# Sinkhorn block attention and token mixer: one stationary matrix for both mixer projections, keys turned by TensorE, the second copy of the queries made by a DMA, and a new order of work with more filler matmuls

## The chip, the cores and the metric

One core of one Trainium2 chip. Times are device microseconds (us) of a whole execution, as medians of several. The profiler's span of one execution is about 1.8 us shorter than its time.

## The reference, cut to what matters

```python
P = sinkhorn(sort_net)                         # per batch (4) and head (8), 8 x 8
k_s = einsum('bhij,bhjcd->bhicd', P, k_b)      # sorted blocks of 96 tokens; v the same
attn = softmax(q_b @ k_s.T / 8)                # inside each block
x = concat_heads(attn @ v_s)                   # 4 x 768 x 512
wq, wk = x @ w_q, x @ w_k                      # 512 -> 64
mixed = einsum('bst,btd->bsd', wq @ wk.T / 8, x)
out = relu(mixed) @ w_out                      # float32
```

## The kernel before

A hand-written order lists units of work; each unit emits its instructions on TensorE (PE), its copy out of PSUM on ScalarE ("a") or VectorE ("d"), and its DMA. The first digit is the batch, the second the part. Q, K, V prepare queries and sorted keys and values; T regroups V by a DMA inside SBUF (VS to VT); S is scores and exponential; AV is the weighted sum; XT transposes; WQ and WK project; A is the small product of wk and x; MIX applies wq; OUT is the last product and the store. A trailing number puts that many filler matmuls, whose results nobody reads, in front of the unit.

```python
ORDER = """
    V00d3 V01a V02d V03a K01d K02a T00 K03a T04 K00d T03 T01 T02 T07 Q12d10 Q13a T06 S00a T05
    S01a S02a Q11d Q10d AV00d AV01d AV02d S03a S05a XT00d AV03d S04a S07a S06a AV04d XT01a V12d
    V11a AV07d WK00a WQ00a AV05d AV06d V13a K13a XT02d K11a ...
"""
# ... loads of inputs, all on GpSimd's queue because they cast float32 to bfloat16 ...
    def further_loads():                     # after the last regroup of batch 0
        load_v(1)
        make_m(1, PTR, nc.gpsimd)
        nc.gpsimd.dma_start(out=wqd[:, :, 0, :], in_=moe_w_q.rearrange("(t p) d -> p t d", p=P))
        nc.gpsimd.dma_start(out=wk_t, in_=moe_w_k.rearrange("(t p) d -> p t d", p=P))
        load_k(1)
        # ... w_out, q2 ...
        nc.gpsimd.tensor_copy(wqd[:, :, 1, :], wqd[:, :, 0, :])      # q weights twice
        # ... v2, k2, q3, v3, k3; three buffers each ...
# ...
    def u_WQ(b, h, eng):                     # q on partitions 0-63 and again on 64-127
        ps = psum1(hf)
        for pt in range(PT):
            nc.tensor.matmul(ps, wqd[:, pt].rearrange("p a d -> p (a d)"),
                             XT[b][:, pt, h * hf:(h + 1) * hf], ...)
        copies[eng](wqT[b][:, h * hf:(h + 1) * hf], ps)

    def u_WK(b, h, eng):                     # keys, tokens on the partitions: 4 x 4 matmuls
        for ii in range(n):
            for pt in range(PT):
                nc.tensor.matmul(ps[0:m, ii, :], XT[b][:, pt, i * BLK:i * BLK + m], wk_t[:, pt, :], ...)
        copies[eng](wkb[b][:, h * n:(h + 1) * n], ps[0:BLK])
```

The softmax here doesn't subtract the row's maximum and nothing guards it: scores larger than these inputs give would overflow.

## Time and profile before

| | before |
|---|---|
| time, median (3 runs) | 114.73 us (113.94 to 115.61) |
| span of the profiled run | 111.7 us |
| mean granted TensorE clock | 0.952 |
| TensorE matmuls | 1444 busy records, 83% of the span |
| ScalarE, VectorE | 67%, 62% |
| DMA engines | full until about 70 us, 0.6 busy to 73 |

In the rows of digits each digit is a fortieth of the span (2.8 us); a 9 is 90% or more. In the table by stretches, columns are busy time and number of instructions of PE, weight loads, VectorE, ScalarE and GpSimd, then clock, DMA share (as printed it can exceed 1) and GB/s. Modelled ends of matmuls overlap, so a unit is priced from one start to the next. The half-clock stretch can also be seen directly: the same AV unit before and inside it, in the timeline (start, duration, engine, line, operation, and in brackets idle time and what ended it):

```profile
24.27 0.44 PE L277 MATMUL ps<-VT,E 96*128 96x65 bf16 x8 [0.25 <-ACT E L265]
...
25.89 0.65 PE L277 MATMUL ps<-VT,E 96*128 96x65 bf16 x8
```

TensorE waits 0.25 us for an exponential, as it does ahead of each AV here; then the clock falls and eight matmuls take half as long again, with no idle time before them.

### The profile page before, as it was taken

To read this page: it belongs to the slowest core of one execution; us is meant where nothing else is said; L and a number is where in the kernel's file an instruction comes from. 1 tells how busy PE (TensorE), PEld (TensorE's weight loads), DVE (VectorE), ACT (ScalarE), POOL (GpSimd) and SP (SyncE) were. 2 spreads that over 40 slices of the span, in tenths; PEclk is the share of its full clock that TensorE was granted. 3 is DMA by queue.
4 is the path that set the end of the run, shared out by engine and by line. 5 is a ranking of instruction groups with operands and counts; after the bars stand their busy time and mean duration, and the time that the engine had idled before them with its cause. 6 is when DMAs were issued, how large, how long until landed. Compare 5 with 4: busy or idle time off the path is not lost.

```text
span 111.7 us, 3418 instructions
## 1 busy us (share of the span) xinstructions
PE 93.2 (83%) x1444; PEld 63.0 (56%) x1444; DVE 68.9 (62%) x154; ACT 75.2 (67%) x116; POOL 33.4 (30%) x54
## 2 busy tenths in 40 slices
PE   0007869977899999999998999999899999999930
PEld 0007326846576787665696688755478687334400
DVE  1586787498365736688897577858388874071000
ACT  4014637578743999849599895995968836885640
POOL 6950002999099900043210000003150000051030
PEclk9999999996555999999999999999999999999999
DMA  0999999999999999999999999602543000048772
GB/s 3 111 202 206 203 203 204 248 132 178 159 193 197 205 204 219 246 239 206 204 216 247 247 368 344 192 4 94 188 183 113 0 0 6 0 164 305 294 269 95
DMA packets 19758, 19.80 MB, mean 177 GB/s; under 512 B 2208, under 2 KB 17696, under 8 KB 19744
## 3 DMA queue, kind: packets, MB, share of 16 engines
q0 software_dynamic: 15696, 15.21, 73.1%
q1 hardware_dynamic: 4048, 4.38, 13.2%
q8 instruction: 11, 0.18, 0.7%
q14 instruction: 3, 0.02, 0.1%
HBM read 20.19 MB, written 6.29 MB: 237 GB/s over the span
## 4 chain that ended last, share of the span: by engine, by line
issue 40%; DMA 29%; POOL 14%; DVE 10%; ACT 1%; PE 1%; POOLq 1%; ACTq 0%
DMA Vn<-in_v_dram 23%; DMA wqd<-in_moe_w_q_dram 6%; POOL out_dram L362 5%; POOL Vn L115 2%; POOL M L217 2%; POOL VT L252 2%; DVE M L217 1%; DVE tmp L162 1%; POOL Qn L105 1%; DVE Pm L161 1%; ACT Pm L155 1%; DVE tmp L160 1%; DVE tmp L163 1%; DVE tmp L159 1%; DVE VS L244 1%
## 5 line engine op out<-in xcount | busy, mean ns | idle before, releaser
L362 POOL DMA_DIRECT2D out_dram<-ot x18 | 9.8, 547 | 59.7 <-ACT ot L360 34.4
L265 ACT ACTIVATE E<-ps 96x768 bf16<-96x768 f32 x32 | 24.0, 810 | 1.4 <-PE ps L260 1.3
L357 PE MATMUL ps<-wo_t,mixT 128*128 128x512 bf16 x96 | 23.1, 379 | 0.0
L284 DVE TENSOR_TENSOR X<-ps,R 96x512 bf16<-96x512 f32 x32 | 22.0, 687 | 1.1
L360 ACT COPY ot<-ps 128x512 f32<-128x512 f32 x20 | 11.8, 588 | 9.0 <-PE ps L357 8.9
L206 PE MATMUL ps<-idb,Qn 128*64 128x128 bf16 x192 | 8.5, 238 | 9.0 <-DMA Qn<-in_q_dram 8.8
L277 PEld LDWEIGHTS <-E 96*128 96x128 bf16 (+1 forms) x256 | 12.4, 108 | 5.2 <-ACT E L265 2.1
L277 PE MATMUL ps<-VT,E 96*128 96x65 bf16 (+1 forms) x256 | 14.0, 204 | 0.8 <-ACT E L265 0.7
L357 PEld LDWEIGHTS <-mixT 128*128 128x128 bf16 x96 | 8.6, 98 | 9.3 <-issue 0.9
L206 PEld LDWEIGHTS <-Qn 128*64 128x64 bf16 x192 | 6.8, 121 | 10.2 <-DMA Qn<-in_q_dram 9.0
L260 PE MATMUL ps<-QT,KT 64*128 64x96 bf16 x256 | 10.0, 211 | 1.4 <-DVE X L284 0.8
L244 ACT CAST VS<-ps 128x768 bf16<-128x768 f32 x11 | 8.8, 827 | 2.9 <-PE ps L241 2.9
L283 DVE RECIPROCAL R<-ps 96x8 f32<-96x8 f32 x32 | 6.3, 198 | 6.7 <-PE ps L277 6.6
L241 PE MATMUL ps<-Vn,M 128*128 128x384 bf16 x32 | 8.1, 361 | 1.7 <-DMA Vn<-in_v_dram 0.9
L260 PEld LDWEIGHTS <-KT 64*128 64x128 bf16 x256 | 7.0, 97 | 4.5 <-issue 1.6
L351 DVE TENSOR_SCALAR mixT<-ps 128x768 bf16<-128x768 f32 x7 | 6.7, 955 | 4.0 <-PE ps L344 3.9
L294 PE MATMUL ps<-idb,X 96*128 96x96 bf16 x128 | 8.3, 211 | 0.0
L234 ACT CAST KT<-ps 128x768 bf16<-128x768 f32 x10 | 7.8, 800 | 0.6 <-PE ps L230 0.5
L230 PE MATMUL ps<-M,Kn 128*64 128x128 bf16 x192 | 7.5, 223 | 0.2 <-DVE VS L244 0.2
L349 ACT ACTIVATE mixT<-ps 128x768 bf16<-128x768 f32 x9 | 7.2, 819 | 0.3 <-PE ps L344 0.3
L230 PEld LDWEIGHTS <-Kn 128*64 128x64 bf16 x192 | 6.1, 112 | 2.1 <-issue 1.0
L294 PEld LDWEIGHTS <-X 96*128 96x128 bf16 x128 | 6.6, 101 | 1.1
(71 smaller groups left out, 128.0 us busy)
## 6 DMA issues: line engine op xcount, KB each, us to landing
out_dram<-ot POOLq DMA_DIRECT2D x18, 256.0 KB, 2.6
Qn<-in_q_dram POOLq DMA_DIRECT2D x4, 768.0 KB, 14.7
Vn<-in_v_dram POOLq DMA_DIRECT2D x4, 768.0 KB, 12.0
Kn<-in_k_dram POOLq DMA_DIRECT2D x4, 768.0 KB, 15.1
VT<-VS SPq DMA_DIRECT2D x28, 97.5 KB, 5.5
out_dram<-ot SPq DMA_DIRECT2D x6, 256.0 KB, 2.0
wo_t<-in_moe_w_out_dram POOLq DMA_DIRECT2D x1, 512.0 KB, 11.7
VT<-VS POOLq DMA_DIRECT2D x4, 97.5 KB, 3.5
```

What stands on the lines that cost most here:

```text
L206: nc.tensor.matmul(ps[hh * D:(hh + 1) * D, r, :], Qn[b][:, 2 * kp + hh, r, :], idb, is_transpose=True, start=True, stop=True, skip_group_c ...
L230: nc.tensor.matmul(ps[hh * D:(hh + 1) * D, r * P:(r + 1) * P], Kn[b][:, h, r, :], Ms[b][:, h].rearrange("p s i -> p (s i)"), start=True, s ...
L241: nc.tensor.matmul(ps[:, hh, 0:R6 * D], Ms[b][:, h].rearrange("p s i -> p (s i)"), Vn[b][:, h].rearrange("p r d -> p (r d)"), start=True, ...
L244: copies[eng](VS[b % 2][:, :, 2 * kp:2 * kp + 2, 0:D].rearrange("p r h d -> p h r d"), ps[:, :, 0:R6 * D].rearrange("p h (r d) -> p h r d" ...
L260: nc.tensor.matmul(ps[:, hh, kp * BLK:(kp + 1) * BLK], KT[b][hh * D:(hh + 1) * D, k0:k0 + P], QT[b][hh * D:(hh + 1) * D, kp, :, i * SP:(i ...
L265: nc.scalar.activation(E.rearrange("p (a n) -> p a n", a=2), ps[0:BLK, :, 0:4 * BLK], ACT.Exp, scale=scale)
L277: nc.tensor.matmul(ps[0:m, h // 4, (h % 4) * D1:(h % 4 + 1) * D1], E[:, e * BLK:e * BLK + m], VT[b][:, i, h, :], start=True, stop=True, sk ...
L284: nc.vector.tensor_mul(Xb[b][:, i].rearrange("p (a t d) -> p a t d", a=2, t=4), pv[:, :, :, 0:D], Rt.unsqueeze(3).to_broadcast([BLK, 2, 4, ...
L294: nc.tensor.matmul(ps[:, pt, ii * BLK:(ii + 1) * BLK], Xb[b][:, 2 * j + ii, pt * P:(pt + 1) * P], idb[0:BLK, 0:BLK], is_transpose=True, st ...
L357: nc.tensor.matmul(ps, mixT[b][:, pt, r, :], wo_t[:, pt, :], start=(pt == 0), stop=(pt == PT - 1), skip_group_check=True)
L360: copies[eng](ot, ps)
L362: queue.dma_start(out=od[:, r, :], in_=ot)
```

## The change

The intent: compute keys and queries in one product (keys on partitions 0 to 63, queries on 64 to 127), turn the keys by four cheap matmuls against the identity, and fetch the second copy of the queries, which MIX needs on partitions 0 to 63, by a DMA inside SBUF (unit "D"). The two weights load right behind q1. The order was searched anew, with units "F" that emit only fillers.

```diff
+    for a, w in ((0, moe_w_k), (1, moe_w_q)):                 # right behind load_q(1)
+        nc.gpsimd.dma_start(out=wkq[:, :, a, :], in_=w.rearrange("(t p) d -> p t d", p=P))
     def further_loads():
-        nc.gpsimd.dma_start(out=wqd[:, :, 0, :], in_=moe_w_q...)
-        nc.gpsimd.dma_start(out=wk_t, in_=moe_w_k...)
-        nc.gpsimd.tensor_copy(wqd[:, :, 1, :], wqd[:, :, 0, :])
     def u_WQ:
-            nc.tensor.matmul(ps, wqd[:, pt]...
+            nc.tensor.matmul(ps, wkq[:, pt]...
+    def u_D(b, n, eng):
+        wq2[b] = rot.tile([DH, S], BF16, tag="wq2", name="wq2")
+        nc.sync.dma_start(out=wq2[b], in_=wT[b][DH:2 * DH, :])
     def u_WK:
-            for pt in range(PT):
-                nc.tensor.matmul(ps[0:m, ii, :], XT[b][:, pt, i * BLK:i * BLK + m], wk_t[:, pt, :], ...
+            nc.tensor.matmul(ps[0:m, ii, :], wT[b][:, i * BLK:i * BLK + m], idb[:, 0:DH], ...
+    def u_F(b, n, eng):
+        psum1(512)
     def u_MIX:
-                             wqv[a * DH:(a + 1) * DH, ...
+                             wqs[a][a * DH:(a + 1) * DH, ...      # wqs = (wq2, wT)
 ORDER: (start of the new one)
+    V00d3 V01a V02d4 V03a K00d K01a K02a T07 K03d T06 T05 T00 Q13d10 Q10a T02 S00a S03a S01a T04
+    Q11d Q12d T01 T03 S05a4 AV00d F002 S02a F024 AV05d S06a AV01d1 F013 AV03d AV02d2 AV06d XT00a
+    S04a1 F044 S07a XT01d AV04d AV07d V13a WQ00a V12a XT02d V10a V11d XT03a WK00d T17 K11a K10d
+    T15 K12a WQ01a T16 T14 K13a D00 WK01d3 T11 S14a4 S16a S10a T13 A00d T12 S17a1 T10 S13a4 S11a4
+    AV17d F172 S12a F124 S15a AV16d MIX00a MIX01a Q21d Q22d ...
```

More of the change, by code (lines that the diff above doesn't have):

```diff
@@ L21 @@
 ORDER = """
-    V00d3 V01a V02d V03a K01d K02a T00 K03a T04 K00d T03 T01 T02 T07 Q12d10 Q13a T06 S00a T05
-    S01a S02a Q11d Q10d AV00d AV01d AV02d S03a S05a XT00d AV03d S04a S07a S06a AV04d XT01a V12d
-    V11a AV07d WK00a WQ00a AV05d AV06d V13a K13a XT02d K11a K12d K10a XT03d V10a S13a1 S14a WQ01d
-    T10 WK01d T12 S17a S12a T11 S11a A00d T14 T16 S16a Q23d Q21d T13 MIX02a MIX01d T17 Q20a Q22d
-    T15 MIX03a MIX00d S10a OUT05a5 AV10d OUT02a AV11d AV12d AV14d OUT01a XT10a V20a V21d OUT03a
-    V23a AV17d V22a OUT04d AV16d AV13d OUT00a T26 T25 K22a T24 K23d XT13a T22 S15a Q31d T23 K21a
@@ L28 @@
-    Q30d T21 K20d Q32a T27 AV15d XT11a T20 S24a2 S20a Q33d S21a WK10d V30d V33a WQ10a V31a AV24d
-    V32a XT12d S22a AV21d T30 S23a WQ11a T32 AV22d AV20d T31 AV23d WK11a T35 K32a T36 A10a1 K30a
-    K31d K33a T37 T33 T34 XT21d XT20a MIX13d MIX12a S34a WK20d3 WQ20a S31a S32a MIX11d OUT15d
-    AV31d OUT13a AV32d OUT14a AV34d MIX10a S30a S33a S25a OUT10d OUT12a AV33d AV25d OUT11a AV30d
-    XT31a S35a XT22d S26a XT30d1 S27a AV35d AV26d WK30a AV27d XT32a S36a WQ30d S37a XT23d AV36d
-    AV37d2 WQ21a WK21a XT33d A20a WQ31a WK31d MIX20a MIX21d MIX22a A30a MIX23a OUT22a OUT21a
@@ L34 @@
-    MIX33d MIX30a MIX32a OUT25d OUT23a MIX31d OUT35a OUT34a OUT32a OUT30a OUT33a OUT31a OUT20a
-    OUT24a
+    V00d3 V01a V02d4 V03a K00d K01a K02a T07 K03d T06 T05 T00 Q13d10 Q10a T02 S00a S03a S01a T04
+    Q11d Q12d T01 T03 S05a4 AV00d F002 S02a F024 AV05d S06a AV01d1 F013 AV03d AV02d2 AV06d XT00a
+    S04a1 F044 S07a XT01d AV04d AV07d V13a WQ00a V12a XT02d V10a V11d XT03a WK00d T17 K11a K10d
+    T15 K12a WQ01a T16 T14 K13a D00 WK01d3 T11 S14a4 S16a S10a T13 A00d T12 S17a1 T10 S13a4 S11a4
@@ new lines @@
+    AV17d F172 S12a F124 S15a AV16d MIX00a MIX01a Q21d Q22d AV11d AV15d XT13a AV13d OUT00a AV12d
+    OUT01a V20a V21d OUT02a V23a XT11d V22a AV10d Q20a Q23d K22a K21d K23a T24 T23 XT10d T21 K20a
+    MIX03d T22 MIX02a WQ10a T20 AV14d T25 S20a S21a T26 OUT03d WK10a T27 S22a S23a S26a Q32d Q33d
+    S24a Q30d AV23d XT12a AV21d OUT05a AV24d AV22d OUT04a V30a AV26d WQ11a V31a V32d XT21a WK11d
+    V33a AV20d D10 S27a Q31d A10a K32a K30d K31a T31 T34 T33 XT20d AV27d T32 MIX10a T35 S25a
+    WQ20d T30 MIX13a MIX11d T36 XT23a AV25d WK20a T37 K33a MIX12d OUT11a XT22d S37a S36a S32a
@@ L36 @@
+    OUT14d AV37d WQ21a AV36d OUT15a WK21d D20 AV32d S34a S33a OUT12d XT33a AV34d S35a S31a A20d
+    S30a AV33d OUT10a AV31d AV30d XT31a AV35d OUT13a MIX23a XT30d MIX22a XT32d WQ30a WQ31a WK30d
+    MIX20a MIX21d D30 WK31a OUT25a A30a OUT20a OUT21a MIX31d MIX33a MIX30a OUT23d OUT22a MIX32d
+    OUT24a OUT32a OUT31a OUT35a OUT34a OUT33a OUT30a
 """
@@ L99 @@
     nc.sync.dma_start(out=Pm[:, 0:NB, :], in_=sort_net.rearrange("b h i j -> (b h) i j"))
+    wkq = const.tile([P, PT, 2, DH], BF16)
     Qn, Kn, Vn = [None] * B, [None] * B, [None] * B
@@ L171 @@
     load_q(1)
-    wqd = const.tile([P, PT, 2, DH], BF16)
-    wk_t = const.tile([P, PT, DH], BF16)
+    for a, w in ((0, moe_w_k), (1, moe_w_q)):
+        nc.gpsimd.dma_start(out=wkq[:, :, a, :], in_=w.rearrange("(t p) d -> p t d", p=P))
     wo_t = const.tile([P, PT, DM], BF16)
@@ L182, in further_loads @@
         make_m(1, PTR, nc.gpsimd)
-        nc.gpsimd.dma_start(out=wqd[:, :, 0, :], in_=moe_w_q.rearrange("(t p) d -> p t d", p=P))
-        nc.gpsimd.dma_start(out=wk_t, in_=moe_w_k.rearrange("(t p) d -> p t d", p=P))
         load_k(1)
@@ L197 @@
     Xb, XT, QT, KT, VT, Ms, Es = {}, {}, {}, {}, {}, {}, {}
-    wqT, wkb, Ab, mixT, ts = {}, {}, {}, {}, {}
+    wT, wq2, wkb, Ab, mixT, ts = {}, {}, {}, {}, {}, {}
     hf = S // 2
@@ L300, in u_WQ @@
     def u_WQ(b, h, eng):
-        if b not in wqT:
-            wqT[b] = rot.tile([P, S], BF16, tag="wqT", name="wqT")
+        if b not in wT:
+            wT[b] = rot.tile([P, S], BF16, tag="wT", name="wT")
         ps = psum1(hf)
         for pt in range(PT):
-            nc.tensor.matmul(ps, wqd[:, pt].rearrange("p a d -> p (a d)"),
+            nc.tensor.matmul(ps, wkq[:, pt].rearrange("p a d -> p (a d)"),
                              XT[b][:, pt, h * hf:(h + 1) * hf],
                              start=(pt == 0), stop=(pt == PT - 1), skip_group_check=True)
-        copies[eng](wqT[b][:, h * hf:(h + 1) * hf], ps)
+        copies[eng](wT[b][:, h * hf:(h + 1) * hf], ps)
+    def u_D(b, n, eng):
+        wq2[b] = rot.tile([DH, S], BF16, tag="wq2", name="wq2")
+        nc.sync.dma_start(out=wq2[b], in_=wT[b][DH:2 * DH, :])
     def u_WK(b, h, eng):
@@ L317, in u_WK @@
             m = P if ii < n - 1 else BLK
-            for pt in range(PT):
-                nc.tensor.matmul(ps[0:m, ii, :], XT[b][:, pt, i * BLK:i * BLK + m], wk_t[:, pt, :],
-                                 start=(pt == 0), stop=(pt == PT - 1), skip_group_check=True)
+            nc.tensor.matmul(ps[0:m, ii, :], wT[b][:, i * BLK:i * BLK + m], idb[:, 0:DH],
+                             start=True, stop=True, skip_group_check=True)
         copies[eng](wkb[b][:, h * n:(h + 1) * n], ps[0:BLK])
+    def u_F(b, n, eng):
+        psum1(512)
     def u_A(b, n, eng):
@@ L338, in u_MIX @@
             mixT[b] = rot.tile([P, PT, R6, P], BF16, tag="mixT", name="mixT")
-        wqv = wqT[b].rearrange("p (i r s) -> p r i s", i=NB, r=R6)
+        wqs = [w.rearrange("p (i r s) -> p r i s", i=NB, r=R6) for w in (wq2[b], wT[b])]
         rh, p2 = n // 2, n % 2
@@ L344, in u_MIX @@
             nc.tensor.matmul(ps[:, a, 0:hf], Ab[b][a * DH:(a + 1) * DH, p2 * P:(p2 + 1) * P],
-                             wqv[a * DH:(a + 1) * DH, rh * nr:(rh + 1) * nr],
+                             wqs[a][a * DH:(a + 1) * DH, rh * nr:(rh + 1) * nr],
                              start=True, stop=True, skip_group_check=True)
@@ L399 @@
     emit = {"Q": u_Q, "K": u_K, "V": u_V, "T": u_T, "S": u_S, "AV": u_AV, "XT": u_XT,
-            "WQ": u_WQ, "WK": u_WK, "A": u_A, "MIX": u_MIX, "OUT": u_OUT}
+            "WQ": u_WQ, "D": u_D, "F": u_F, "WK": u_WK, "A": u_A, "MIX": u_MIX, "OUT": u_OUT}
     for kind, b, n, eng, m in re.findall(r"([A-Z]+)(\d)(\d)([ad]?)(\d*)", ORDER):
```

## The prediction

> **What bounds the kernel now.** I read four views. First the page's busy shares and its 40 slices:
>
> ```profile
> PE 93.2 (83%) x1444; PEld 63.0 (56%) x1444; DVE 68.9 (62%) x154; ACT 75.2 (67%) x116; POOL 33.4 (30%) x54
> PE   0007869977899999999998999999899999999930
> PEclk9999999996555999999999999999999999999999
> DMA  0999999999999999999999999602543000048772
> ```
>
> TensorE is busy to the end, but three slices (2.8 us each) run at half its clock, and the DMA engines are full until about 73 us. Second, the table by stretches, cut where the clock changes (engine columns PE, PEld, DVE, ACT, POOL, then clock, DMA share, GB/s):
>
> ```profile
> 14.90:20.40 5.50, 4.68 (x66) 3.00 (x66) 4.59 (x7) 3.40 (x5) 1.68 (x4) 1.00 1.25 210
> 20.40:25.90 5.50, 4.63 (x122) 3.72 (x121) 3.97 (x9) 3.77 (x6) 5.50 (x6) 1.00 0.95 179
> 25.90:35.90 10.00, 8.92 (x102) 6.36 (x102) 5.32 (x13) 5.33 (x9) 7.22 (x9) 0.50 1.34 182
> 35.90:95.40 59.50, 58.22 (x1045) 41.99 (x1045) 43.26 (x84) 48.24 (x74) 9.74 (x15) 1.00 0.81 176
> 95.40:107.10 11.70, 11.66 (x58) 4.74 (x56) 2.61 (x3) 8.31 (x15) 2.15 (x4) 1.00 0.56 209
> ```
>
> Exactly 10 us are at clock 0.50. Third, the waits:
>
> ```profile
> POOL wqd L188 <- DMA wqd<-in_moe_w_q_dram: 2.8, 1, 2.8
> PE ps L241 <- DMA Vn<-in_v_dram: 0.9, 2, 0.5
> PEld L230 <- DMA Kn<-in_k_dram: 0.7, 1, 0.7
> ```
>
> These PE waits are short, but they mark gates: batch 1's v arrives at 30.1 us, its k at about 35.7, batch 3's v at 61.5. Fourth, the timeline, to price a piece of work by start-to-start distances, since a modelled matmul time (190 ns for 64 columns) overlaps its neighbours:
>
> ```profile
> 85.59 0.69 PE L319 MATMUL ps<-wk_t,XT 128*128 128x64 bf16 x16
> ...
> 86.12 0.44 PE L277 MATMUL ps<-VT,E 96*128 96x65 bf16 x8
> ```
>
> A WK unit (16 matmuls) really costs 86.12 - 85.59 = 0.53 us, 33 ns a matmul; in the half-clock stretch the same unit takes 0.96 us (31.82 to 32.78). Priced in this way at full clock: Q, K, V 0.33 us, S and AV 0.27, XT 0.35, WQ 0.65, A 0.85, MIX 0.2, OUT 0.86, a filler matmul 0.107. The whole order is then 77.2 us of TensorE work, spread over 14.9 to 107.1 us = 92.2 us. So TensorE is the bound, at 84%. Of the 15 us lost, the half-clock stretch loses the most: from 25.9 to 35.9 us the units add up to only 4.7 us. From batch 1's K units (35.8 us) to the start of batch 3's (67.5) it does 28.6 us of work in 31.7 us (90%); from there 36.0 in 39.6 (91%).
>
> **What the skill says.** "TensorE: Matmul & The Clock Gate", Part 1, says that the clock is gated to half or full by activity over windows of about 3.4 us. Three windows are 10.2 us; the stretch here is 10.0, which agrees. The page warns of idle gaps longer than a window; no such gap is here (TensorE shows 4.63 of 5.5 us busy just before), so the trace contradicts a rule of idle gaps only[...]. Part 4 adds that transposes do not count as busy in the same way; 25.4 us does hold one, but no run so far isolates that. The same page, "Back-to-back issue gap", gives about 25 ns as the floor of a matmul of up to 64 columns; the trace has 33 ns with its weight load. "DMA: Bandwidth & Descriptors", section on SWDGE, HWDGE and iDMA, says that a casting DMA must be issued from GpSimd. The weights are cast from float32, so they share GpSimd's queue with q, k and v, and their place in it matters.
>
> **The change part by part.**
>
> WK. The q and k projections now share one stationary matrix, at no extra cost, because WQ already computed q twice. WK becomes 4 matmuls against the identity instead of 16. There are 8 units: 96 matmuls and 96 weight loads go. At 33 ns each this is 3.2 us at full clock (0.53 to 0.13 us a unit). It lengthens one path: WK now waits for the WQ copy (0.48 us on ScalarE). The order puts other units between.
>
> The doubling DMA. Four copies of 64 x 1536 B = 96 KB on SyncE's queue, about the size of the VT regroups (97.5 KB), whose landing took 3.0 / 5.4 / 7.2 us (least, median, most) mostly under load. Between WQ11 and MIX10 stand some 4.8 us of TensorE work and ScalarE work besides, between WQ31 and MIX31 about 4.1 us with idle DMA engines (a landing at the low end, 3 us, is my estimate). So I take them as hidden, with 0 to 0.5 us leaking.
>
> Weights behind q1. In the kernel before they were issued at 23.6 and 24.4 us, behind v1, and k1 waited behind them. q1 is used at 20.4 us and v1 is only issued at 20.8: the DMA engines have a hole there (their share falls from 1.25 to 0.95 in the second stretch). The weights fall into it. They landed at 30.4 and 30.9 us against 30.1 for v1, so they took roughly 0.8 us of the stream. k1 should land about 1 us earlier, near 34.8. The GpSimd copy of wqd and its 2.8 us wait go as well, but the queue behind it is full of loads anyway, so I give nothing for it. The cost: the four regroups that GpSimd issues now queue behind the weights and land about 1 us later; the new order asks for them later (four S units instead of three ahead of AV00).
>
> Fillers. They grow from 28 to 60, +32 x 0.107 = 3.4 us of TensorE work, nearly as much as WK saves. All lie in batches 0 and 1: 38 in batch 0 (13 before), 21 of them among its S and AV units, where TensorE waited for the exponentials (737 ns each on ScalarE), and 22 in batch 1. They should fill the thin windows before 25.9 us and keep the clock up. That, rather than the 3.2 us, is what I count on.
>
> The order. Adding up my prices along both orders, the work standing ahead of each gate is: K1 12.6 us before, 15.9 after; V3 35.8 and 41.4; K3 41.2 and 45.8; total 77.2 and 77.5. The change thus puts about 4.6 us more work ahead of batch 3's keys.
>
> **The sum.** Stage 1: at the k1 gate, 34.8 us, the changed kernel can have done its 15.9 us if the clock stays up; after v1 lands at about 30 it has only 2.7 us of work left to there, so it even waits a little. Stage 2: K1 to K3 is 45.8 - 15.9 = 29.9 us. At 90% it takes 33.0 us. But ScalarE's work in that part, priced from its mean times, rises from 29.2 to 31.6 us; before it filled 92% of the 31.7 us, and at 92% it takes 34.3. So K3 starts at 67.8 to 69.1, against 67.5 before, with k3 landed by then. Stage 3: 77.5 - 45.8 = 31.7 us at 91% is 34.9 us, so the last OUT ends at 102.7 to 104.0 instead of 107.1. The last store leaves by SyncE (2.0 us to landing) rather than GpSimd (2.6): 0.3 us. The gain is 3.4 to 4.7 us: 114.7 becomes 110.0 to 111.3. I take **110.6**.
>
> **Rivals.** (a) The clock drops anyway, for instance in the wait for k1 between about 33 and 34.8 us. One cold window costs about half its length, 1.7 us; three cost 4 to 5. The time would be 112.3 to 114.5. For it: the kernel before went cold at 84% busy. Against it: the added fillers stream 256 columns each. (b) ScalarE becomes the bound: 74.7 us of priced work against 73.3, with exponentials bunched in batch 1 (eight in a row, 5.9 us). TensorE's saving then comes out as idle time, and the result is about 112. The 67% busy share speaks against it, the 92% in the middle for it. (c) Input loads pace batch 3: k3 cannot land much before 66 us. The new order has put more ahead of it, so this only limits a gain above about 6 us. (d) Regroups or doubling copies land late: each stall costs up to 2 us, and the time goes back to 113 to 114.
>
> **Range and chances.** The limit for faster is 114.73 x 0.98 = 112.4. Main path with (b) in part gives 110 to 111.3; (a) in full or (d) twice gives about 114. The kernel before itself spread from 113.94 to 115.61, perhaps by the phase of the clock window. I give the clock three chances in four, hence faster 0.74, within 2% 0.20, slower 0.06, with 108.0 to 113.8 as the range.
>
> **What would show it.** The clock row should have no fives at slices 10 to 12; if it has, the main step fails. WK units should measure about 0.13 us start to start. The first K of batch 1 should start at 34 to 35.5 us and be released by k's load; the first of batch 3 at 67 to 69.5. ScalarE should be above 90% between them. The last OUT matmul should end near 103.5. A wait of MIX on the doubled q above 1 us, or of AV on VT, would confirm (d). The prediction is wrong above all if TensorE stays warm and the time still hardly moves.

## The result

The changed kernel takes 109.07 us (median of 4, 108.56 to 109.57), the kernel before 114.40 (4 runs in the same comparison). The ratio is 0.952 (95% interval 0.943 to 0.961). Ratios are the mean time of one kernel's fast runs over that of the other's of the same rounds, so not quite the ratio of the medians. Repeated beside the later experiments it was 108.47 us (0.947) and 108.44 us (0.945).

The page of the changed kernel, with the rows that answer those of before:

```profile
PE 89.5 (84%) x1371; PEld 60.3 (56%) x1380; DVE 66.7 (62%) x153; ACT 76.2 (71%) x117; POOL 33.0 (31%) x53
PE   0006887999999899699999999989999999999960
PEclk9999999999999999999999999999999999999999
DMA  0999999989999999999999999846144222155784
```

The fives are gone from the clock row; the dip in the PE row in slice 17 (counting from 1, 42.7 to 45.4 us) is new and holds the first wait below. The table by stretches, cut at the first K of batch 1, the first K of batch 3 and the last OUT matmul:

```profile
14.90:35.10 20.20, 18.44 (x321) 13.38 (x319) 15.26 (x31) 13.63 (x20) 15.44 (x16) 1.00 1.22 192
35.10:68.60 33.50, 32.15 (x587) 23.55 (x592) 23.02 (x48) 29.43 (x44) 3.57 (x7) 1.00 1.25 241
68.60:103.10 34.50, 33.72 (x415) 19.78 (x416) 19.69 (x38) 27.07 (x44) 6.48 (x12) 1.00 0.45 153
```

The three waits that matter, from its waits (total, times, longest):

```profile
PE ps L348 <- DMA wq<-wT: 1.4, 2, 0.9
PE ps L228 <- DMA Kn<-in_k_dram: 0.4, 1, 0.4
DVE wT L306 <- DMA VT<-VS: 0.6, 1, 0.6
```

The first is new: MIX waits for the doubled queries of batches 0 and 1 (0.94 and 0.47 us). The second is the gate of batch 1's keys (0.40 us in the third run of this kernel, none in the second). The third, VectorE's on a regroup, was 0.6 us before too. No wait on v is left. The WK unit, priced from start to start in the timeline, is now 66.31 - 66.18 = 0.13 us:

```profile
66.18 0.30 PE L320 MATMUL ps<-idb,wT 128*128 128x64 bf16 x4
66.31 0.33 PE L239 MATMUL ps<-Vn,M 128*128 128x384 bf16 x1
```

Milestones, read off the timelines of TensorE (us from the span's start):

| | first V, batch 0 | first K, batch 1 | first V, batch 3 | first K, batch 3 | end of last OUT matmul | span |
|---|---|---|---|---|---|---|
| before | 14.90 | 35.83 | 61.55 | 67.55 | 107.06 | 111.7 |
| changed | 15.48 | 35.07 | 63.94 | 68.62 | 103.13 | 106.8 |
| changed, second chip run | 14.91 | 33.99 | 63.48 | 68.16 | 102.64 | 106.3 |
| changed, third | 15.09 | 34.63 | 63.73 | 68.41 | 103.09 | 106.9 |

The changed kernel reaches batch 3's v and k later than before. It has done more by then (batch 3's v comes after 41.4 us of priced work instead of 35.8), and what remains is shorter: 34.5 us against 39.5.

### The profile page after: what moved, and what is told of

The parts are those of the page before. It is cut to its first block, busy times and chain, and to the rows that moved or that the text cites. A ratio compares the mean times of both kernels' runs of the same rounds, so it can differ in the third digit from the quotient of the medians.

```text
span 106.8 us, 3286 instructions
## 1 busy us (share of the span) xinstructions
PE 89.5 (84%) x1371; PEld 60.3 (56%) x1380; DVE 66.7 (62%) x153; ACT 76.2 (71%) x117; POOL 33.0 (31%) x53
## 4 chain that ended last, share of the span: by engine, by line
PE 49%; DMA 24%; DVE 8%; ACT 7%; issue 4%; POOL 3%; ACTq 0%; POOLq 0%
PE ps L361 20%; DMA wq<-wT 12%; DMA Kn<-in_k_dram 10%; PE ps L275 5%; PE ps L348 4%; PE ps L292 4%; PE ps L303 3%; DMA VT<-VS 3%; PE ps L204 3%; PE ps L258 3%; PE ps L228 2%; PE ps L331 2%; PE ps L239 2%; ACT KT L232 2%; ACT VS L242 2%
## 5 line engine op out<-in xcount | busy, mean ns | idle before, releaser
L275 PE MATMUL ps<-VT,E 96*128 96x65 bf16 (+1 forms) x256 | 13.4, 196 | 0.2 <-ACT E L263 0.2
L275 PEld LDWEIGHTS <-E 96*128 96x128 bf16 (+1 forms) x256 | 11.6, 101 | 2.8 <-ACT E L263 0.3
L84 PE MATMUL ps<-ones,idb 128*128 128x256 bf16 x60 | 9.8, 280 | 0.9 <-ACT PTR L400 0.6
L258 PE MATMUL ps<-QT,KT 64*128 64x96 bf16 x256 | 9.2, 204 | 0.0
L353 ACT ACTIVATE mixT<-ps 128x768 bf16<-128x768 f32 x10 | 7.8, 813 | 1.5 <-PE ps L348 1.5
L232 ACT CAST KT<-ps 128x768 bf16<-128x768 f32 x11 | 8.4, 813 | 0.6 <-PE ps L228 0.4
L296 ACT COPY XT<-ps 128x768 bf16<-128x768 bf16 x8 | 6.5, 813 | 2.3 <-PE ps L292 2.3
L355 DVE TENSOR_SCALAR mixT<-ps 128x768 bf16<-128x768 f32 x6 | 5.7, 954 | 3.9 <-PE ps L348 3.8
L258 PEld LDWEIGHTS <-KT 64*128 64x128 bf16 x256 | 6.3, 94 | 2.8 <-issue 1.7
L228 PE MATMUL ps<-M,Kn 128*64 128x128 bf16 x192 | 7.0, 220 | 0.8 <-DMA Kn<-in_k_dram 0.4
## 6 DMA issues: line engine op xcount, KB each, us to landing
VT<-VS SPq DMA_DIRECT2D x28, 97.5 KB, 6.0
VT<-VS POOLq DMA_DIRECT2D x4, 97.5 KB, 3.1
```

Of the source, the lines that this page charges most:

```text
L84: nc.tensor.matmul(t, idb, ones[:, 0:256], start=True, stop=True, skip_group_check=True)
L232: copies[eng](KT[b][:, kp * S:(kp + 1) * S].rearrange("p (i s r) -> p i s r", i=NB, r=R6), ps[:, 0:S].rearrange("p (r s i) -> p i s r", r= ...
L258: nc.tensor.matmul(ps[:, hh, kp * BLK:(kp + 1) * BLK], KT[b][hh * D:(hh + 1) * D, k0:k0 + P], QT[b][hh * D:(hh + 1) * D, kp, :, i * SP:(i ...
L275: nc.tensor.matmul(ps[0:m, h // 4, (h % 4) * D1:(h % 4 + 1) * D1], E[:, e * BLK:e * BLK + m], VT[b][:, i, h, :], start=True, stop=True, sk ...
```

## The experiments

Twelve runs were made, in three sets on one chip each (first two sets on one chip, the third on another). All were correct. The first set had no run of the changed kernel beside it; its members are compared by their ratio to the kernel before, as the changed kernel's 0.945 to 0.952 is. "Slow" here is a run more than 1.5% above the fastest of the same kernel. In the first set six of the nine runs of the kernel before were slow, so its ratios rest on few. The medians take in slow runs too; the fast runs alone have these means: changed kernel 108.03 us in both repetitions, g1 108.01, f2 109.26 (two runs only), g3 109.28, f3 110.99, g2 113.31, f1 118.38.

| run | what it is | median us | ratio to before (95%) | clock of profile |
|---|---|---|---|---|
| e1_after_few_fillers | changed, 13 fillers instead of 60 | 112.32 | 0.987 (0.979 to 0.996) | 0.923 |
| e2_before_with_fillers | before, 25 fillers added | 115.14 | 1.005 (0.993 to 1.017) | 0.996 |
| e3_after_old_wk | changed, old WK, no doubling DMA | 110.15 | 0.966 (0.957 to 0.975) | 1.000 |
| e4_after_late_weights | changed, weights behind v1 | 109.95 | 0.960 (0.948 to 0.972) | 0.981 |
| f0_after_again | changed | 108.47 | 0.947 (0.940 to 0.953) | 1.000 |
| f1_new_body_old_order | new parts in the old order | 118.71 | 1.038 (1.031 to 1.044) | 0.965 |
| f2_mix_later | changed, three MIX units later | 110.90 | none given | 1.000 |
| f3_fillers_batch0_only | changed, 38 fillers | 111.34 | 0.973 (0.966 to 0.979) | 0.965 |
| g0_after_third | changed | 108.44 | 0.945 (0.938 to 0.952) | 0.997 |
| g1_regroups_behind_copy | changed, copy earlier in its queue | 108.86 | 0.947 (0.939 to 0.955) | 0.994 |
| g2_q_doubled_by_pe | changed, q doubled by TensorE | 113.47 | 0.994 (0.988 to 0.999) | 1.000 |
| g3_late_weights_again | e4 again | 109.66 | 0.958 (0.951 to 0.965) | 0.980 |

### The fillers in the changed order

```diff
-  V02d4 ... S05a4 AV00d F002 S02a F024 AV05d S06a AV01d1 F013 AV03d AV02d2 ... S04a1 F044 ... S14a4 ...
+  V02d  ... S05a  AV00d      S02a      AV05d S06a AV01d       AV03d AV02d  ... S04a       ... S14a  ...
```

> The changed kernel with 13 fillers instead of 60 (only the three ahead of V00 and the ten ahead of Q13 stay; the F units go). Clock theory: the fillers are what keeps TensorE's clock up; the clock row shows two to four slices near half (mean clock at or below 0.97) somewhere between 25 and 45 us, and the time is 110.5 to 113 us. Rival, that WK's lighter arithmetic and the new order carry the gain: the clock stays at 1.00 or its drop costs nothing because batch 1's keys gate TensorE anyway, and the time is 108 to 109.5 us.

Measured: 112.32 us, ratio 0.987. Two stretches of its table by stretches:

```profile
26.00:36.00 10.00, 9.79 (x101) 6.92 (x99) 6.43 (x15) 5.37 (x8) 8.38 (x8) 0.51 1.29 202
46.30:53.00 6.70, 6.45 (x73) 4.56 (x74) 3.91 (x9) 2.61 (x4) 0.00 (x0) 0.51 1.29 218
```

The clock halves in the same place as in the kernel before, and a second time in batch 1's attention, where the kernel before did not fall. Forty-seven filler matmuls that compute nothing are worth 3.5 to 4% here: 0.987 against 0.945 to 0.952. All five runs had a mean clock of 0.923 to 0.939. The clock theory holds in the changed order.

### The fillers of batch 1 alone

```diff
-  WK01d3 T11 S14a4 ... S17a1 T10 S13a4 S11a4 AV17d F172 S12a F124 S15a
+  WK01d  T11 S14a  ... S17a  T10 S13a  S11a  AV17d      S12a      S15a
```

> The changed kernel without the 22 fillers of batch 1; the 38 of batch 0 stay. Clock theory: the run with few fillers went cold a second time at about 46 us; here too the clock falls once, near 43 to 48 us, for 3.4 us or more, and the time is 0.7 to 2 us more than the changed kernel. Rival: those fillers only fill idle time, the clock stays at 1.00 and the time is within 0.3 us.

Measured: 111.34 us, all six runs between 110.28 and 112.62, against 108.47 (107.42 to 110.01) on the same chip. So these 22 fillers carry about 2.9 us, more than I expected. The clock fell in all six runs, the four fast ones too: 0.962 to 0.978, against 0.992 to 1.000 in the six of the changed kernel beside it. Its profile was a slow run; it shows one half-clock stretch, in batch 1 (44.5 to 51.4 us), as e1's fast profile does at 46.1 us. Since the kernel with all fillers but these is 2.9 us slower and the one with hardly any 3 to 4 us, the second fall of the clock is the larger part of the two in the changed order. That split is a comparison of sets, not a measured sum.

### The fillers in the old order

```diff
-  AV00d AV01d AV02d S03a S05a XT00d AV03d S04a S07a S06a AV04d XT01a V12d
+  AV00d2 AV01d2 AV02d2 S03a S05a2 XT00d AV03d2 S04a3 S07a S06a5 AV04d3 XT01a V12d4
```

> The kernel before with 25 fillers added among the S, AV and V units of batch 0 and nothing else. Clock theory: no half-clock stretch, mean clock 0.99 or 1.00; but k of batch 1 still lands near 35.7 us and holds TensorE there, so only part of the 4.7 us of work done at half speed comes back: 112 to 113.2 us. Rival, that the clock is worth all of the gain: 109 to 111 us. Rival, that the clock is worth nothing: 114 to 115 us.

Measured: 115.14 us, ratio 1.005. The clock is full (0.996), and nothing is gained; even my cautious figure missed. In TensorE's timeline the reason stands at batch 3's first V:

```profile
62.85 0.81 PE L241 MATMUL ps<-Vn,M 128*128 128x384 bf16 x4 [1.59 <-DMA Vn<-in_v_dram]
```

Batch 1's first K starts at 35.26 us instead of 35.83, so most of the 4.7 us of work done at half clock before had been hidden behind the load of batch 1's keys. The rest is given back 27 us later, where TensorE now waits 1.59 us for batch 3's v (0.43 before). That load was also issued 0.6 us later (35.9 against 35.3 us) and landed 1.3 us later (62.7 against 61.4), so an earlier TensorE could not help. The clock was worth nothing while the order tied TensorE to the loads. The kernel before says the same by itself: two of its executions in the later sets had a mean clock of 1.000, and they took 114.54 and 114.44 us, no less than its medians there (114.26 and 114.35).

### The new parts in the old order

```diff
+  (bodies and weight loads of the changed kernel)
-  V11a AV07d WK00a WQ00a ... S13a1 S14a WQ01d T10 WK01d
+  V11a AV07d WQ00a WK00a ... S13a1 S14a WQ01d D00 T10 WK01d      (and 25 fillers as in the last run)
```

> The new body (joint projection, identity turn, doubling copy, early weights) in the order of the kernel before (each WK moved behind its WQ, a doubling copy behind each second WQ), with 25 fillers in batch 0 so that the clock stays up. Gate theory: the old order has only some 35 us of work ahead of batch 3's v, which lands at 61 to 63 us whatever TensorE does, so V3 waits 1 us or more for it and the time is 112.5 to 115 us. Rival, that the parts carry the gain and the order is only a detail: 109 to 111.5 us.

Measured: 118.71 us, ratio 1.038: slower than the kernel before, worse than any theory gave. The old order puts WK right behind WQ in most places, with little room for the copy out of PSUM and for the doubling DMA: by the prediction's prices 2.7 us of work stand between the first doubling copy and the first MIX, 6.0 in the new order. That this is the cause is argued from the order. The profile, of a slow run, shows waits for both (WK on the copy of wT, and the first MIX on the DMA). The fillers did not keep the clock wholly up (0.976 to 0.997 in the fast runs), but the run at 0.997 still took 117.60 us, so the clock is not what makes it slow. In the old order the parts lose 3.8%, and in the order searched for them the kernel gains 5%. The order, which the diff hardly invites to read, is what makes the parts pay. It changes both the sequence and which engine copies each unit out ("a" or "d"); no run separates these two.

### The WK arithmetic

```diff
-            nc.tensor.matmul(ps[0:m, ii, :], wT[b][:, i * BLK:i * BLK + m], idb[:, 0:DH], ...
+            for pt in range(PT):
+                nc.tensor.matmul(ps[0:m, ii, :], XT[b][:, pt, i * BLK:i * BLK + m], wk_t[:, pt, :], ...
   (q weights twice, no D units, MIX reads both halves of wT)
```

> The changed kernel with WK computed as before (16 matmuls against a k weight of its own, q computed twice, no doubling copy), in the changed order and with its fillers and early weights. Arithmetic theory: TensorE gets 8 x 0.40 = 3.2 us more work, less the 1.4 us that MIX waits for the doubled q: 110.5 to 112 us. Rival, ScalarE is the bound from batch 1's keys on and the TensorE time saved turns into idle time: 108.5 to 109.7 us.

Measured: 110.15 us, ratio 0.966; 1.1 to 1.7 us more than the changed kernel's medians. Its two last stretches:

```profile
34.94:68.95 34.01, 33.59 (x628) 24.79 (x628) 23.35 (x48) 29.79 (x44) 4.08 (x7) 1.00 1.22 237
68.95:104.45 35.50, 35.50 (x468) 21.39 (x464) 19.79 (x37) 27.15 (x43) 6.49 (x12) 1.00 0.40 137
```

From batch 1's first K to the last OUT it takes 34.01 + 35.50 = 69.5 us, the changed kernel 103.13 - 35.07 = 68.1. Seven of the eight WK units lie there: 7 x 0.40 = 2.8 us of TensorE work. The changed kernel's two waits on the doubling DMA are 1.4 us. 2.8 - 1.4 = 1.4 us is the whole difference. On this sum the TensorE time saved became elapsed time, and half of it was paid out again for the DMA. That is argued, not shown: it is one profile against another, the time lies between the two ranges told, and a run below takes 1.2 us of that wait away without a clear gain. What the ratio does show is more: with the old arithmetic the new order, its fillers and the early weights reach 0.966 alone, so they carry about 3.4 of the 5%.

### How q is doubled

```diff
-        nc.sync.dma_start(out=wq2[b], in_=wT[b][DH:2 * DH, :])
+        for h in range(2):
+            ps = psum1(hf)
+            nc.tensor.matmul(ps[0:DH], idb[:, DH:2 * DH], wT[b][:, h * hf:(h + 1) * hf], ...)
+            nc.vector.tensor_copy(wq2[b][:, h * hf:(h + 1) * hf], ps[0:DH])
```

> The changed kernel with q doubled by TensorE and VectorE (for each batch two matmuls against the identity's upper half and two copies of 64 x 384) instead of the DMA. It adds 8 x 0.16 = 1.3 us of TensorE and 8 x 0.56 = 4.5 us of VectorE work and takes away the waits of MIX on the DMA (1.4 us). If the DMA is a clear win: 1 to 2.5 us slower than the changed kernel. If its waits eat what it saves: within 0.6 us of it. No wait of MIX on a DMA in either case.

Measured: 113.47 us (112.76 to 113.68), 5.0 us more than the changed kernel beside it: nearly the whole gain is lost, twice what I allowed. The copies take 0.54 us each on VectorE as priced, 8 in all; the loss is spread over the kernel. Against the third run of the changed kernel the stretch from batch 1's first K to batch 3's is 1.5 us longer and the rest 2.4 us. (The first K of batch 1 comes 0.8 us later too, at 35.43, but no doubling stands ahead of it; this profile has a wait of 0.78 us for a regroup at 27.7 us.) Each doubling needs two PSUM buffers of the small pool in turn:

```profile
PE ps L324 <- DVE wq L314: 1.1, 1, 1.1
PE ps L204 <- DVE wq L314: 0.6, 1, 0.6
```

These are a WK and a Q unit waiting for VectorE's copy of a doubling, presumably for the PSUM buffer that it holds. They are 1.7 us of the 3.9; for the rest no wait is shown. The DMA, late as it is, occupies no compute engine and no PSUM.

### Hiding the wait for the doubled q, twice

By moving MIX:

```diff
-  AV16d MIX00a MIX01a Q21d Q22d AV11d AV15d          and   MIX10a T35 S25a WQ20d T30 MIX13a
+  AV16d Q21d Q22d AV11d MIX00a MIX01a AV15d          and   T35 S25a WQ20d T30 MIX10a MIX13a
```

> The changed kernel with MIX00 and MIX01 placed three units later and MIX10 three units later, so that the doubled q has landed. If the 0.94 and 0.47 us that TensorE waited there count: no wait on the doubled q above 0.2 us and 0.4 to 1.3 us less than the changed kernel on this chip. If other engines or the input loads take the time up again: within 0.3 us of it.

Measured: 110.90 us with a wide scatter (109.09 to 113.21), against 108.47 beside it: a miss. The two fast runs (109.26 us in the mean) are still 1.2 us above the changed kernel's fast runs. The fast profile shows why it does not gain. The waits on the DMA are gone, but AV units wait in their place:

```profile
44.03 0.43 PE L275 MATMUL ps<-VT,E 96*128 96x65 bf16 x8 [0.49 <-DMA VT<-VS]
45.63 0.45 PE L275 MATMUL ps<-VT,E 96*128 96x65 bf16 x8 [0.38 <-DMA VT<-VS]
47.25 0.43 PE L275 MATMUL ps<-VT,E 96*128 96x65 bf16 x8 [0.74 <-ACT mixT L353]
```

Two wait for regroups, 0.87 us together, and one is released by ScalarE's copy of the shifted MIX, so presumably waited for the PSUM buffer that it held. The two fast runs kept their clock (1.000), the four slow ones had 0.981 to 0.984; that goes with the longer times, but 110.82 and 112.86 us at nearly the same clock show that it is not all, and why they go up to 113 us stays open.

By moving the copy ahead in its queue:

```diff
-  WK00d T17 K11a K10d T15 K12a WQ01a T16 T14 K13a D00 WK01d3 T11 S14a4 S16a
+  WK00d T17 K11a K10d T16 K12a WQ01a K13a D00 WK01d3 T11 S14a4 T15 S16a ... T14 T10
```

> The changed kernel with two of the four regroups of batch 1 (T15 and T14) moved behind the doubling copy of batch 0 in SyncE's queue. If the copy is late because four regroups of 97.5 KB stand before it in its queue: it lands 1.5 to 2.5 us sooner after its issue, the wait of MIX00 is under 0.3 us, and the time is 0.4 to 1.2 us less than the changed kernel. If the input loads make it late: landing still near 7 us and the time within 0.3 us. Rival from the previous try: the wait moves to AV on a later regroup and the time is not less.

Measured: the copy of batch 0 lands 5.6 us after its issue instead of 7.1, so the regroups ahead of it in SyncE's queue were a cause (one profile; the three of the changed kernel have 7.0 to 7.3). TensorE's wait of 1.16 us for it at 45 us in the run beside it is gone. The two views of the waits on it, the third run of the changed kernel and this one:

```profile
PE ps L348 <- DMA wq<-wT: 1.8, 2, 1.2
```

```profile
PEld L348 <- DMA wq<-wT: 0.5, 1, 0.5
```

The profiled run ends its last OUT at 102.51 us instead of 103.09. But the medians are 108.86 and 108.44 and the ratios 0.947 and 0.945, whose intervals overlap almost wholly; the fast runs alone have means of 108.01 and 108.03 us. The gain of 0.4 to 1.2 us that I told is not there. Whether the wait was worth anything stays open; it is less than about 0.8 us. No version beat the changed kernel.

### The place of the weight loads

```diff
-    (two loads into wkq behind load_q(1))
+    (the same two loads inside further_loads, behind load_v(1) and make_m)
```

> The changed kernel with the two weight loads back behind v1. Gate theory: k1 lands about 1 us later, the first K of batch 1 starts at about 36 instead of 35.1 us, and the time is 109.5 to 110.3 us. Rival, the order of the loads is hidden: within 0.4 us of the changed kernel (108.7 to 109.5).

> The changed kernel with the two weight loads back behind v1, tried again because the first try scattered over 3 us. Gate theory: the first K of batch 1 starts 0.4 to 1.5 us later than in the changed kernel and the time is 0.4 to 1.5 us more. Rival: the loads' place is hidden and the time is within 0.3 us.

Measured: 109.95 us (108.49 to 111.60) and, tried again, 109.66 us (108.87 to 111.44), ratio 0.958 against 0.945 beside it. So the place is worth about 1.2 us of medians, the size I gave it; the two intervals (0.951 to 0.965, 0.938 to 0.952) just touch. Both profiles fell on slow runs, each with one stretch of 3.4 us at half clock that the changed kernel lacks, but not in the same place (from 46.8 us in the first, from 33.7 in the second). The fast runs of the second try had a clock of 0.993 to 1.000 and were still 1.2 us slower, so the clock is not what the place costs. The gate that I named is not shown either: the first K of batch 1 started at 35.46 us in the first profile, with 0.3 us of wait on k. One wait in the second profile is a candidate that I had not named:

```profile
34.07 1.44 PE L303 MATMUL ps<-XT,wkq 128*128 128x384 bf16 x4 [1.52 <-DMA wkq<-in_moe_w_q_dram]
```

Batch 0's first WQ waits for its own weights: in the new order WQ comes early and its weights can gate it. The first profile, of the same kernel, has no such wait, so through what the time goes stays open.

## Why the prediction was right

The time (110.6 told, 109.07 measured) lies in the range and the class is right. Point by point:

- **Stages.** Batch 1's K at 34.8 told, 34.0 to 35.1 measured; batch 3's K at 67.8 to 69.1 told, 68.2 to 68.6 measured; last OUT at 102.7 to 104.0 told, 102.6 to 103.1 measured. Pricing units from start to start and adding them along the order carried this. (The waits on the doubled q lie inside the told lengths, so the other work ran about 1 us closer together than the 90 and 91% that I took; that these two cancel is luck.)
- **Clock.** It stayed up, through the fillers (e1). The price that I put on it in the kernel before was wrong: I let the half-clock stretch lose the most of TensorE's time, but there a full clock gains nothing (e2, and the two executions of the kernel before at 1.000), because the loads of batch 1's k and batch 3's v gate it. I named the gates, yet expected 1.2 to 2.4 us from e2. The same two executions speak against the phase of the clock window, which I guessed to be behind the spread of the kernel before. What I had not seen: 22 of the fillers prevent a second fall that the kernel before does not have.
- **WK.** 0.13 us a unit as told. By the sum under e3, 2.8 us of it reach the elapsed time between batch 1's K and the end, before the DMA's waits; that is argued from two profiles.
- **Doubling DMA.** Told 0 to 0.5 us of leak, measured 1.4 in each of the first two profiles and 1.8 in the third. The failed step is the landing time: 4.8 us of work stood between WQ11 and MIX10, and I did not do the same sum for batch 0, where 6.0 us of work at the same prices stand between D00 and MIX00, while four regroups of 97.5 KB are issued before the copy and it took 7.0 to 7.3 us to land.
- **ScalarE.** Told above 90% from batch 1's K to batch 3's; measured 29.43 of 33.50 us, 88%. It is near the bound, not at it. The 92% that I gave the kernel before was a sum of mean times, and these overlap: its busy time there is 27.25 of 31.72 us, 86%.
- **The tail.** Told 0.3 us from the last store's queue; measured 1.0. From the last OUT matmul to the end of the span it is 4.6 us before and 3.7 after. That is a mis-sized term of the sum: 0.7 of the 1.5 us by which the time came out under 110.6. Another is the start: every stage was read from a profiled run of 113.44 us, but the gain was taken off the median of 114.73, 1.3 us more. Together they make 2.0 us; the profiled run of the changed kernel in turn lay 0.5 us under its median (108.56 against 109.07). The tail goes with the order: it is 4.6 us in the profiles of all three kernels in the old order, whose last two stores leave by GpSimd, and 3.7 to 4.0 in all those in the new one. No run isolates the queue from the rest of the order.
- **Rivals.** (a) did not happen in the changed kernel but is what removing fillers brings; (b) was mild; (c) did not happen: in the old order batch 3's v does gate (e2), but the new one moves 5.6 us of work ahead of it, so that the load is no longer waited for; (d) happened at 1.4 us, without the stalls of 2 us.

## What to carry to other kernels

Price a saving in the order in which it will stand: list the gates that other engines set (here the landings of k1 and v3) and the work placed before each, because a faster engine in front of a gate only waits. TensorE fillers cost little where it would idle and can be worth several per cent when they keep its clock up, but only if the time they give back is not behind such a gate. A DMA that copies inside SBUF costs no compute engine, but count what stands before it in its queue.

## What the Trainium skill lacked or had wrong

- "TensorE: Matmul & The Clock Gate", Part 1 and the table at the page's end, warn of idle gaps of about 3 us. Here the clock halved with TensorE busy by the profile in 4.63 of the 5.5 us before, and no single idle piece of its matmuls above 0.26 us between 20.4 and 25.9 us. The page's section "A second HAM failure mode: psum-queue depth-cycling", which the prediction passed over, does tell of short idles between groups of matmuls that let the clock swing; it gives no threshold of activity. The window of about 3.4 us agrees: summed from the clock column in slices of half a microsecond, the stretches at half clock are 10.24 us in the kernel before (10.0 in the prediction), 10.24 and 6.82 in e1, 6.83 in f1 and f3, 3.42 and 3.41 in e4 and g3: one, two or three windows. Adding 256-column fillers to the gaps kept the clock up (e1 against the changed kernel). No run isolates whether transposes count; besides the XT that the prediction names, the Q units at 20.4 and 21.8 us are transposes too.
- The same page, "Back-to-back issue gap", gives about 25 ns as the floor for matmuls of up to 64 columns, and for pairs of weight load and matmul only figures at 128 and 512 columns; at 64 columns with a weight load each it was 33 ns (0.53 us for 16, 0.13 us for 4).
- "DMA: Bandwidth & Descriptors", "Anatomy of one DMA — SWDGE (gpsimd) path", fits 2.0 us plus bytes over 436 GB/s (2.2 us for 96 KB by estimate, though for the other path). The copy on SyncE's queue took 2.1 us with idle DMA engines and 7.0 to 7.3 us with input loads running and four regroups queued before it, 5.6 with two. The page has no figure for a DMA behind others.
- No page gives the spread between whole executions: one kernel took 107.42 to 110.01 us in six runs.
